# Whole weight rows with the step inside the staging tile, numerators beside keys, and weight passes tied behind chosen places of the first attention

## The chip, the cores and the metric

The kernel runs on one core of a Trainium2 chip. The metric is the device time of one execution in microseconds (us), median of several runs. The engines are called as the profile calls them: PE (TensorE matmul), PEld (its weight loads), DVE (VectorE), ACT (ScalarE), POOL (GpSimd) and SP (SyncE, which issues the loads here). The clock is PE's mean granted clock, 1.00 being full.

## The reference, cut to what matters

Four batches, four heads, 1088 positions, head size 32. An attention with squared sketch features gives `x` of 1088 x 128; a wave mixing multiplies its cosine and sine parts by two 1088 x 1088 weights.

```python
def phi(x):                                   # r = 8, so 64 features a head
    a = np.einsum('rd,bhsd->bhsr', S1, x)
    b = np.einsum('rd,bhsd->bhsr', S2, x)
    return np.einsum('bhsi,bhsj->bhsij', a, b).reshape(*x.shape[:-1], r * r)
num = phi(q) @ (phi(k)^T v)                   # shortened
den = phi(q) @ sum(phi(k)) + 1e-06
x = num / den
...
zr, zi = x * np.cos(x @ w_theta), x * np.sin(x @ w_theta)
y = np.einsum('ts,bsd->btd', w_tok_r, zr) + np.einsum('ts,bsd->btd', w_tok_i, zi)
u = x + y
return u + np.maximum(u @ w_ch, 0.0)
```

The weights arrive as float64 and are carried in as int64 bits. They must become f32 on the chip: 17 rows of 128 x 1088, each 8 bytes a value.

## The kernel before: the parts that matter

A weight piece is turned into f32 by three ACT passes and two DVE passes. ACT writes a scaled float of the high word, and beside it a 4-byte "step" made of an int16 (from the low word) and an f16 (from the high word); DVE shifts the float's bits by three and adds the step.

```python
def load_f32(dst, src):                       # PIECE = 544 columns
    st = stg.tile([P, PIECE], I64, tag="st", name="st")[:p, :n]
    nc.sync.dma_start(st, src)
    lo, hi = split(st)
    step = stg.tile([P, PIECE, 2], I16, tag="step", name="step", bufs=2)[:p, :n]
    x = dst.bitcast(I32)
    A.activation(dst, hi.bitcast(F32), AF.Copy, scale=2.0**-112)
    A.activation(step[:, :, 1].bitcast(F16), hi.bitcast(F32), AF.Copy, scale=2.0**-60)
    A.activation(step[:, :, 0], lo.bitcast(U32), AF.Copy, scale=2.0**-29)
    ts(x, x, 3, ALU.logical_shift_left)
    tt(V, x, x, step.rearrange("p n t -> p (n t)").bitcast(I32), ALU.add)
```

A scheduler puts the instructions of all stages in order on each engine by priority when the kernel is built.

```python
# ... end of the first attention, priority "first"
    query_slices(0); matrices(0); keys_values(0, spare); attention(0)
with level("attention"):
    keys(1); attention(1); keys(2)
mixing(0, True)
with level("attention"):
    attention(2); keys(3)
mixing(1, False)
# ... attention(3), mixing(2), mixing(3)
```

## Time and profile before

| | before |
|---|---|
| time, median (lowest to highest) | 358.53 us (357.6 to 360.12, 4 runs) |
| span, mean PE clock of the profiled run | 357.9 us, 0.877 |
| PE busy, DVE busy, ACT busy | 274.9, 250.4, 153.8 us |
| first mixing matmul | 115.87 us |
| last weight row ready | 117.4 us |
| second attention's denominators begin on DVE (fl) | 160.38 us |
| mixing of batch 1 begins | 189.55 us |

The last four rows of the table are milestones of the execution. One is fl, the first DVE instruction of the second attention that needs its features. This is it in the timeline of the kernel before (start, duration, engine, line, operation, tiles; in brackets the idle time before it and its releaser):

```profile
160.38 1.06 DVE L100 SCALAR_TENSOR_TENSOR fl<-lv 128x864 f32<-128x864 f32 x1 [2.07 <-ACT lv L449]
```

And this is the busy time on each side of it (PE, PEld, DVE, ACT, POOL, clock, DMA share, GB/s):

```profile
0.00:160.38 160.38, 90.69 (x447) 66.02 (x448) 124.57 (x405) 102.37 (x188) 0.70 (x6) 0.78 0.46 154
160.38:357.90 197.52, 184.19 (x910) 126.08 (x908) 125.88 (x309) 51.46 (x125) 0.00 (x0) 0.96 0.07 21
```

After fl, PE is busy for 184 of 197.5 us. Before it, no engine is: DVE for 125 and ACT for 102 of 160.

### The profile page before, as it was taken

The numbers are of one execution on the slowest core, as the hardware profiler recorded it, in microseconds if no ns is written. First come the engines' busy times: TensorE is split into PE (matmuls) and PEld (weight loads), VectorE is DVE, ScalarE is ACT, GpSimd is POOL, SyncE is SP. The second block draws the span as 40 slices with busy tenths as digits, with TensorE's granted clock in tenths as the row PEclk, the third lists the DMA queues.
The fourth block names the chain that finished last, engine by engine and source line by source line (L and its number), as shares of the span: only waits on it lengthen the run. The fifth ranks groups of instructions, "written<-read, shape, count | busy, mean of one in ns | idle before, by whom it ended". The sixth has DMA issues, their size and how long they took to land.

```text
span 357.9 us, 4021 instructions
## 1 busy us (share of the span) xinstructions
PE 274.9 (77%) x1355; PEld 192.1 (54%) x1355; DVE 250.4 (70%) x713; ACT 153.8 (43%) x313; POOL 0.7 (0%) x6
## 2 busy tenths in 40 slices
PE   0406680145327999999689999996999999999994
PEld 0304480023226676776357777674777766776562
DVE  4898886985996699559948794896589569542111
ACT  0799729997958442061134413312335131332000
POOL 0000000000000000000000000000000000000000
PEclk9999955556555899999969999997899999999998
DMA  7668447883720012020010122000000000000010
GB/s 289 214 229 269 153 145 243 293 304 108 238 59 4 2 65 69 0 67 3 22 40 2 65 66 70 21 22 20 0 0 3 0 9 15 22 20 0 0 44 18
DMA packets 11604, 28.78 MB, mean 80 GB/s; under 512 B 1216, under 2 KB 5568, under 8 KB 11584
## 3 DMA queue, kind: packets, MB, share of 16 engines
q1 hardware_dynamic: 11376, 28.51, 24.3%
q8 instruction: 10, 0.16, 0.2%
q14 instruction: 10, 0.08, 0.1%
q10 hardware_dynamic: 208, 0.02, 0.0%
HBM read 26.30 MB, written 2.23 MB: 80 GB/s over the span
## 4 chain that ended last, share of the span: by engine, by line
PE 69%; DVE 17%; ACT 8%; DMA 3%; issue 1%; ACTq 0%
PE y L566 36%; PE w L519 4%; PE acc L398 3%; ACT step L135 3%; PE w L539 2%; PE y L576 2%; PE y L398 2%; PE w L446 2%; ACT step L136 2%; DVE wT L93 2%; PE w L513 2%; PE w L388 2%; DMA s_t_st<-s_t 2%; PE acc L306 2%; PE w L447 2%; PE w L534 1%
## 5 line engine op out<-in xcount | busy, mean ns | idle before, releaser
L566 PE MATMUL y<-wT,zst 128*128 128x384 f32 (+1 forms) x384 | 134.8, 481 | 1.4 <-DVE zst L93 1.4
L566 PEld LDWEIGHTS y<-wT,zst 128*128 128x128 f32 x384 | 68.1, 193 | 30.6 <-DVE zst L93 2.3
L585 ACT COPY ot<-y 128x384 f32<-128x384 f32 (+2 forms) x16 | 6.0, 398 | 62.1 <-PE y L580 62.1
L135 ACT ACTIVATE step<-st 128x544 f16<-128x544 f32 (+1 forms) x35 | 27.8, 795 | 4.3 <-DVE wT L93 4.2
L93 DVE CUSTOM_DVE_ANT_0 wT<-wT,step 128x1088 uint16<-128x1088 uint16 x34 | 24.4, 718 | 5.8 <-ACT step L136 5.8
L519 PEld LDWEIGHTS w<-kvbd,qpT 128*128 128x128 f32 x144 | 21.6, 213 | 11.3 <-ACT qpT L517 10.4
L136 ACT ACTIVATE step<-st 128x544 int16<-128x544 uint32 (+1 forms) x35 | 27.4, 784 | 0.0
L519 PE MATMUL w<-kvbd,qpT 128*128 128x64 f32 x144 | 23.4, 297 | 3.2 <-ACT qpT L517 3.1
L134 ACT ACTIVATE wT<-st 128x544 f32<-128x544 f32 x34 | 22.9, 685 | 2.3 <-DMA st<-w_tok 2.2
L517 ACT COPY qpT<-w 128x256 f32<-128x256 f32 x36 | 12.9, 367 | 24.6 <-PE w L513 24.5
L513 PE MATMUL w<-ident,qp 128*128 128x128 f32 x72 | 14.6, 304 | 7.7 <-DVE qp L93 7.6
L93 DVE TENSOR_TENSOR uT<-xT,y 128x384 f32<-128x384 f32 (+1 forms) x12 | 6.3, 529 | 19.2 <-PE y L566 19.1
L97 DVE TENSOR_SCALAR tn<-w 128x384 f32<-128x384 f32 x12 | 6.7, 557 | 17.8 <-PE w L539 17.8
L536 ACT COPY xT<-w 128x384 f32<-128x384 f32 x12 | 5.7, 475 | 29.8 <-PE w L534 29.8
L449 ACT COPY lv<-w 128x384 f32<-128x384 f32 x36 | 14.9, 504 | 8.3 <-PE w L448 8.2
L513 PEld LDWEIGHTS w<-ident,qp 128*128 128x128 f32 x72 | 10.1, 170 | 9.8 <-ACT wT L134 8.1
L97 DVE TENSOR_SCALAR wT<-wT 128x544 int32<-128x544 int32 x34 | 14.6, 435 | 0.0
L446 PE MATMUL w<-mv,q 128*128 128x384 f16 x36 | 13.4, 372 | 0.8 <-DVE mv L93 0.8
L398 PEld LDWEIGHTS acc<-ld_v,kp 128*128 128x128 f32 x108 | 13.0, 192 | 1.5
L539 PEld LDWEIGHTS w<-w,xT 128*128 128x128 f32 x72 | 10.6, 215 | 5.2 <-ACT xT L536 4.5
L404 ACT COPY kvbd<-acc 64x64 f32<-64x64 f32 x6 | 1.2, 206 | 27.6 <-PE acc L398 27.6
L100 DVE SCALAR_TENSOR_TENSOR fl<-lv 128x864 f32<-128x864 f32 x4 | 4.2, 1054 | 12.3 <-ACT lv L449 12.3
(230 smaller groups left out, 523.5 us busy)
## 6 DMA issues: line engine op xcount, KB each, us to landing
st<-w_tok SPq DMA_DIRECT2D x34, 544.0 KB, 4.6
ld_k<-k_l SPq DMA_DIRECT2D x4, 576.0 KB, 4.0
ld_q<-q_l SPq DMA_DIRECT2D x4, 576.0 KB, 4.4
ld_v<-v_l SPq DMA_DIRECT2D x4, 576.0 KB, 3.8
out<-ot SPq DMA_DIRECT2D x8, 192.0 KB, 2.1
out<-ot SPq DMA_DIRECT2D x4, 128.0 KB, 1.8
st<-w_sq SPq DMA_DIRECT2D x1, 256.0 KB, 4.6
out<-ot SPq DMA_DIRECT2D x4, 32.0 KB, 1.8
```

The costliest lines, as they stand in the source:

```text
L93: eng.tensor_tensor(out=o, in0=a, in1=b, op=op)
L97: V.tensor_scalar(out=o, in0=a, scalar1=s1, scalar2=s2, op0=op0, **kw)
L134: A.activation(dst, hi.bitcast(F32), AF.Copy, scale=2.0**-112)
L135: A.activation(step[:, :, 1].bitcast(F16), hi.bitcast(F32), AF.Copy, scale=2.0**-60)
L136: A.activation(step[:, :, 0], lo.bitcast(U32), AF.Copy, scale=2.0**-29)
L398: nc.tensor.matmul(kv[:, n], kp[:, i * H + 2 * n:i * H + 2 * n + 2].rearrange("p h i j -> p (h i j)"), vn[:, c, 2 * n:2 * n + 2].rearrange ...
L446: nc.tensor.matmul(lp, q0, flat[:, 0:4 * W], start=True, stop=False, skip_group_check=True)
L449: A.copy(lv[:, :, :, c].rearrange("p l t n -> p (l t) n"), lp.rearrange("p (x n) -> p x n", n=HR))
L513: nc.tensor.transpose(tr[:, n * P:(n + 1) * P], qp[:, i * H + 2 * n:i * H + 2 * n + 2].rearrange("p h i j -> p (h i j)"), ident)
L519: nc.tensor.matmul(num[:, i * P + n * 2 * D:i * P + (n + 1) * 2 * D], qpT[:, n], kvbd[b][:, n], start=True, stop=True)
L539: nc.tensor.matmul(th[:, i * P:(i + 1) * P], xT[:, i * P:(i + 1) * P], w2[:, 0], start=True, stop=True)
L566: nc.tensor.matmul(yp[:, :t1 - t0], z, wT[:, i, t0:t1], start=(i == 0), stop=(i == NK - 1))
```

## The change

Its intent is to save instruction issues (whole rows in place of halves), to save memory (the step is written inside the staging tile), and to let PE begin the mixing earlier (half of the first batch's numerators runs beside its keys, and the weight passes on DVE are held behind places of the first attention). The core of the diff, cut:

```diff
-        st = stg.tile([P, PIECE], I64, tag="st", name="st")[:p, :n]
+        st = stg.tile([P, S], I64, tag="st", name="st")[:p, :n]
-        step = stg.tile([P, PIECE, 2], I16, tag="step", name="step", bufs=2)[:p, :n]
+        step = st.bitcast(I16).rearrange("p (n t) -> p n t", t=4)
         A.activation(dst, hi.bitcast(F32), AF.Copy, scale=2.0**-112)
+        A.activation(step[:, :, 0], lo.bitcast(U32), AF.Copy, scale=2.0**-29)
         A.activation(step[:, :, 1].bitcast(F16), hi.bitcast(F32), AF.Copy, scale=2.0**-60)
-        A.activation(step[:, :, 0], lo.bitcast(U32), AF.Copy, scale=2.0**-29)
         ts(x, x, 3, ALU.logical_shift_left)
-        tt(V, x, x, step.rearrange("p n t -> p (n t)").bitcast(I32), ALU.add)
+        rows.append(last_on_dve())
+        tt(V, x, x, lo, ALU.add)
+        rows.append(last_on_dve())
 ... # pool "stg": bufs 4 -> 3; key and query slices share one buffer; z of batch 0 has its own
-        query_slices(0)
-        matrices(0)
-        keys_values(0, spare)
-        attention(0)
+        matrices(0)
+        n_ready = tiles["ready", 0]
+        gates.extend([n_ready] * 2)
+        query_slices(0)
+        features_s(0)
+        denominator_slices(0, 1, 2)
+        keys_values(0, spare)
+        nums = [numerator(0, g, spare) for g in range(NG)]
+        features_n(0)
+        denominator_slices(0, 2, 3)
+        denominators(0)
+        gate(2)
+        d_ready = last_on_dve()
+        for g in range(NG):
+            mixed(0, g, nums[g])
+            gate(1 if g == 0 else NK)
+        for i, ins in enumerate(rows):
+            tc.add_manual_dep(ins, gates[i // 2].name, ...)
     with level("attention"):
-        keys(1)
+        with tc.issue_after(n_ready):
+            load(1, "kqv"); keys_powers(1); query_powers(1)
+        with tc.issue_after(d_ready):
+            keys(1)
```

Below, the *ties* are the `add_manual_dep` loop, and the *hold* is the pair of `issue_after` blocks.

## The prediction

> **What bounds the kernel now.** I read the page's busy table first, then its slices, then the start of the first mixing matmul in the timeline, then busy time by stretch, then the groups.
>
> The busy table and the slices (engine, then tenths of each 8.95 us):
>
> ```profile
> PE 274.9 (77%) x1355; PEld 192.1 (54%) x1355; DVE 250.4 (70%) x713; ACT 153.8 (43%) x313; POOL 0.7 (0%) x6
> ...
> PE   0406680145327999999689999996999999999994
> ...
> DVE  4898886985996699559948794896589569542111
> ACT  0799729997958442061134413312335131332000
> ```
>
> There are two stages. For about 13 slices (to 116 us) PE is idle more than half the time while DVE and ACT are loaded; after that PE is at 9 nearly everywhere. The border is the first matmul of the token mixing (line 566), in the timeline:
>
> ```profile
> 115.73 0.55 DVE L93 TENSOR_TENSOR zst<-x,tt 128x384 f32<-128x384 f32 x1
> 115.87 0.50 PEld L566 LDWEIGHTS y<-wT,zst 128*128 128x128 f32 x2 [1.42 <-DVE zst L93]
> 115.87 2.92 PE L566 MATMUL y<-wT,zst 128*128 128x384 f32 x4 [1.23 <-DVE zst L93]
> ```
>
> It waits for DVE (zst, end of the first attention's first group), not for a weight. The busy times by stretch (us, PE, PEld, DVE, ACT, POOL, PE clock, DMA share, GB/s) say what kept DVE:
>
> ```profile
> 60.00:70.00 10.00, 1.05 (x7) 0.69 (x6) 9.47 (x29) 9.93 (x17) 0.00 (x0) 0.50 0.87 309
> 70.00:80.00 10.00, 3.78 (x15) 2.11 (x16) 8.84 (x44) 9.98 (x17) 0.00 (x0) 0.50 0.85 298
> ...
> 90.00:100.00 10.00, 4.53 (x18) 3.63 (x18) 10.00 (x17) 8.71 (x17) 0.00 (x0) 0.50 0.61 198
> ...
> 120.00:130.00 10.00, 10.00 (x71) 7.76 (x71) 5.94 (x16) 4.19 (x9) 0.00 (x0) 1.00 0.00 0
> ```
>
> Before 116 us the conversion of the token weights (int64 bits to f32) shares DVE and ACT with the first attention. Its groups, 34 pieces of 544 columns for 17 weight rows:
>
> ```profile
> L135 ACT ACTIVATE step<-st 128x544 f16<-128x544 f32 (+1 forms) x35 | 27.8, 795 | 4.3 <-DVE wT L93 4.2
> L93 DVE CUSTOM_DVE_ANT_0 wT<-wT,step 128x1088 uint16<-128x1088 uint16 x34 | 24.4, 718 | 5.8 <-ACT step L136 5.8
> L136 ACT ACTIVATE step<-st 128x544 int16<-128x544 uint32 (+1 forms) x35 | 27.4, 784 | 0.0
> L134 ACT ACTIVATE wT<-st 128x544 f32<-128x544 f32 x34 | 22.9, 685 | 2.3 <-DMA st<-w_tok 2.2
> L97 DVE TENSOR_SCALAR wT<-wT 128x544 int32<-128x544 int32 x34 | 14.6, 435 | 0.0
> ```
>
> Later marks from the timeline: the last value that features(0) needs (mv) is ready at 77.6 us; mixing(0) ends on PE at 172.5; DVE starts the second attention's denominators (fl) at 160.4; mixing(1) starts at 189.55, and from there 168.3 us remain, nearly all PE.
>
> [...] four mixing matmuls take 2.92 us at 115.9, later ones 0.64 a pair, and the clock column reads 0.50 at 60 to 80.
>
> **The change, part by part.**
>
> 1. Whole rows. A row was six ACT instructions; in the timeline they start every 0.57, 0.67 and 0.65 us, so 2 x 1.89 = 3.8 us. Whole rows save three issues. [...] 3.6 us a row (estimate; [...] 4.1 if writing every 8 bytes is dearer). ACT total changes by 17 x 0.2 = 3 us only. DVE: 2 x (0.35 + 0.63) = 2.0 becomes 0.64 + 1.2 = 1.85 (estimate)[...].
>
> 2. Order. The instruction order of the changed kernel shows no weight pass on DVE until the first batch's numerator matrix is ready (call it N), then two rows, two around the end of the denominators, one after group 0 and twelve after that. Of the 33.5 us of weight passes (34 x 0.98, starts) some 21 sat before 77.6 us. Numerators beside keys put the half features, their slices and three qp products before N, and 36 numerator matmuls on PE. Walking the chain, with durations of the same operations in the timeline of before: s_t arrives 2 to 3 us earlier (it is issued ahead of q and v), so the scales are known near 14 us (14.7 now) and the key slices start at 15.6 (18.5 now) and take 5.3 (0.67 + 1.27 + 0.67 + 0.67 + 1.27, with small operations between): 20.9. The S matrices' cut (ten small, 1.8), their product and its scale (3.2) open PE's key sums at 26, which take 5.6 as now (31.3 to 37.3): 31.5. The query slices (4.7) and the cut of the key matrix (4) share DVE: 41. Half features on PE and ACT: 42. Then DVE has three kp (0.88 each), three qp (0.88), one batch column of slices (some 4) and the small operations of the matrix, paced by PE's transposes and products between them: 59. The last twenty dependent small operations cost 0.2 each: N = 63, if PE gets full clock after the half features. At half clock the 18 value and 36 numerator products (0.22 to 0.25 an instruction in place of 0.11 to 0.13) cost some 7 us more: N = 70.
>
> 3. From N: two rows (3.7), the rest of the denominators and two maxima of the next batch, 17 to 18 us of DVE: 81. Group 0 through x, theta, sine, zst: 10 us more. First mixing matmul near 91 to 92, 24 us earlier than now.
>
> 4. But the rows come later. With three staging buffers only rows 0 to 2 can pass ACT before N. Rows 3 and 4 follow at N + 8 to N + 15; row 5 stands behind the sine of group 0 on ACT (91), rows 6 and 7 behind the sines of groups 1 and 2. Row 7 ends near 105 and nine rows remain from 107. Each costs ACT 3.6 plus 0.5 of other work. The buffer loop is as long: add 1.3, DMA about 5.7 (4.6 for half the bytes; at 300 GB/s 0.56 MB more is 1.9), ACT 3.6, some DVE queueing, over three buffers 3.9. I take 4.2 a row: 9 x 4.2 = 38, so the last row is ready at E = 145.
>
> 5. After E. [...] the second attention's last matrix operations stand behind row 16's add: mixing(0)'s tail, one kp, the matrix, about 10.5 us; features on PE and ACT 5; then the denominators, 20 us of DVE as now (the key slices of batch 2 now stand inside them, because the shared slice buffer delays them), and 7 us of sine chain: mixing(1) at 145 + 42 = 187. Before: 189.55. The remainder is the same work in nearly the same order: 187 + 168 = 355 span, 1 us more by the clock.
>
> So of 24 us won at the start, 22 come back as a wait for weights and an exposed second attention. PE's idle time moves from before 116 us to 145 to 187.
>
> **The rivals.** (a) PE is the only bound from the first mixing matmul on: then the 24 us stay, 335. For it: PE at 9 after 116 us. Against: weights were finished by then; now they are not. [...] (b) [...] (c) PE stays cold through the numerators, N = 70: 362. For it: the 36 value matmuls at 46 to 54 us ran at half clock for 8 us without release; against: after the key sums (to 37 us) full clock held at half load until PE fell idle.
>
> **Range and chances.** The sum gives 355 to 356; a (partly) pulls down by 5 to 20, b and c push up by 6 to 8. I shade to 354, because every place of the ties looks chosen so that the model's mixing never starves, and I may have overdrawn the loop. Range 343 to 366. Faster than 351.7: 0.38; slower than 366: 0.12; between: 0.50.
>
> **What would show it.** First mixing matmul at 88 to 96 (part 3); whole-row ACT passes of 1.1 to 1.4 us and adds of 1.2 (part 1[...]); the last row's add at 140 to 150 and PE waiting for DVE's wT between 100 and 145 (part 4); PE mostly idle for 20 to 25 us before mixing(1), near 187 (part 5). The prediction is wrong if the rows end before 130 us, or if the second attention's features no longer wait for the last row.

The forecast's sum came to 355 to 356 us, shaded to 354. The slopes per column behind the 3.6 us a row put a 2-byte pass at 1.3 us, the branch of rival (a) ended at 350 us, and rival (b) made 364 us of dearer stores and a dearer add. The 4.1 us a row for dearer stores is a guess that names no source. The 3.6 can be followed from the kernel before: its ACT passes have a form of 256 columns beside that of 544, and the differences give 0.96 ns a column for f32 (409 and 685 ns) and 1.16 for the 2-byte outputs (460 and 793, 471 and 804). With 544 columns more, starts every 0.57, 0.67 and 0.65 us become 1.09, 1.30 and 1.28: 3.7 us a row (estimate).

## The result and the profile after

| | before | after |
|---|---|---|
| time, median (lowest to highest) | 358.53 us | 393.76 us (392.71 to 394.78, 4 runs) |
| span, mean PE clock | 357.9 us, 0.877 | 391.8 us, 0.843 |
| PE busy, DVE busy, ACT busy | 274.9, 250.4, 153.8 us | 293.7, 251.0, 191.3 us |
| first mixing matmul | 115.87 us | 95.65 us |
| last weight row ready | 117.4 us | 179.8 us |
| fl of the second attention | 160.38 us | 196.58 us |
| span after fl | 197.5 us | 195.2 us |

The changed kernel is 9.8% slower: ratio 1.0977, 95% interval 1.0927 to 1.1027. A ratio here is the mean time of one kernel's fast runs over that of the other's of the same rounds, so it is not quite the ratio of the medians.

First the page of the changed kernel: busy time, then tenths in 40 slices of 9.8 us, and PE's clock.

```profile
PE 293.7 (75%) x1382; PEld 203.2 (52%) x1382; DVE 251.0 (64%) x673; ACT 191.3 (49%) x263; POOL 0.7 (0%) x6
...
PE   2265889207967384467913999999799999999994
...
ACT  1997212596998999992611235051134341043000
...
PEclk9996655555898777858975799999999999999999
```

PE does start earlier, and then never gets going: its digits are ragged until about 215 us. In slices 10 to 17, counted from 0 (98 to 176 us), ACT stands at 9 nearly throughout. ACT's busy time grew by 37.5 us, though it has 50 instructions fewer. The groups name the growth (count, busy us, mean ns of one, idle us before them and releaser):

```profile
L145 ACT ACTIVATE st<-st 128x1088 int16<-128x1088 uint32 (+1 forms) x18 | 45.5, 2528 | 0.0
L146 ACT ACTIVATE st<-st 128x1088 f16<-128x1088 f32 (+1 forms) x18 | 45.4, 2520 | 0.3
L103 DVE CUSTOM_DVE_ANT_0 wT<-st,wT 128x2176 uint16<-128x2176 uint16 x17 | 21.9, 1289 | 21.7 <-ACT st L146 21.6
L144 ACT ACTIVATE wT<-st 128x1088 f32<-128x1088 f32 x17 | 20.6, 1209 | 4.4 <-DMA st<-w_tok 4.4
```

The f32 pass (L144) and the add (L103) cost about what was predicted (1.1 to 1.4 and 1.2), 1.2 and 1.3 us. The two 2-byte passes, L145 and L146, cost 2.5 us and not 1.1 to 1.4. The means mix in one short form of 256 columns; of the 17 full rows alone they are 2632 and 2624 ns. DVE waits 21.6 us for the second of them. The last row in the timeline shows the chain, and how an operation of the second attention (mxn) stands behind it:

```profile
95.65 1.65 PE L618 MATMUL y<-wT,zst 128*128 128x384 f32 x2 [1.59 <-DVE zst L103]
...
173.21 2.62 ACT L145 ACTIVATE st<-st 128x1088 int16<-128x1088 uint32 x1
...
175.86 2.62 ACT L146 ACTIVATE st<-st 128x1088 f16<-128x1088 f32 x1
...
177.23 0.27 PE L360 MATMUL acc<-ident,mn 128*1 128x128 f32 x1
178.51 1.29 DVE L103 CUSTOM_DVE_ANT_0 wT<-st,wT 128x2176 uint16<-128x2176 uint16 x1 [1.57 <-ACT st L146]
179.72 0.27 DVE L362 TENSOR_REDUCE mxn<-acc 1x4 f32<-1x128 f32 x1
...
196.58 1.06 DVE L110 SCALAR_TENSOR_TENSOR fl<-lv 128x864 f32<-128x864 f32 x1 [1.48 <-ACT lv L464]
...
223.56 0.91 PE L618 MATMUL y<-wT,zst 128*128 128x384 f32 x2
```

Row follows row every 6.1 to 6.2 us (the f32 pass of the last four starts at 153.59, 159.74, 165.95 and 172.09). The line at 223.56 is the first of batch 1's mixing. The span on each side of fl tells where the 33.9 us come from:

```profile
0.00:196.58 196.58, 121.58 (x520) 84.31 (x520) 126.27 (x369) 140.79 (x142) 0.70 (x6) 0.75 0.36 128
196.58:391.80 195.22, 172.12 (x862) 118.89 (x862) 124.73 (x305) 50.49 (x122) 0.00 (x0) 0.94 0.06 18
```

Before fl there are 36.2 us more (196.58 less 160.38), after it 2.3 fewer. DVE did the same work before fl (126 us against 125). ACT did 38 us more (141 against 102). So all of the loss lies before the second attention's denominators.

### The profile page after: what moved, and what is told of

Its sections match the earlier page's. It is cut to its first block, busy times and chain, and to the rows that moved or that the text cites. A ratio compares the mean times of both kernels' runs of the same rounds, so it can differ in the third digit from the quotient of the medians.

```text
span 391.8 us, 3966 instructions
## 1 busy us (share of the span) xinstructions
PE 293.7 (75%) x1382; PEld 203.2 (52%) x1382; DVE 251.0 (64%) x673; ACT 191.3 (49%) x263; POOL 0.7 (0%) x6
## 4 chain that ended last, share of the span: by engine, by line
PE 52%; ACT 26%; DVE 17%; issue 2%; DMA 2%; SPq 0%; ACTq 0%; DVEq 0%
PE y L618 24%; ACT st L145 9%; ACT st L146 9%; ACT wT L144 4%; PE acc L415 3%; PE w L566 2%; PE w L591 2%; PE w L560 2%; PE w L405 2%; PE y L415 2%; PE y L628 2%; DVE lv L103 2%; DVE wT L103 1%; DVE ksl L110 1%; DMA st<-w_tok 1%
## 5 line engine op out<-in xcount | busy, mean ns | idle before, releaser
L618 PE MATMUL y<-wT,zst 128*128 128x384 f32 (+1 forms) x408 | 154.2, 512 | 22.1 <-DVE wT L103 20.5
L146 ACT ACTIVATE st<-st 128x1088 f16<-128x1088 f32 (+1 forms) x18 | 45.4, 2520 | 0.3
L145 ACT ACTIVATE st<-st 128x1088 int16<-128x1088 uint32 (+1 forms) x18 | 45.5, 2528 | 0.0
L103 DVE CUSTOM_DVE_ANT_0 wT<-st,wT 128x2176 uint16<-128x2176 uint16 x17 | 21.9, 1289 | 21.7 <-ACT st L146 21.6
L144 ACT ACTIVATE wT<-st 128x1088 f32<-128x1088 f32 x17 | 20.6, 1209 | 4.4 <-DMA st<-w_tok 4.4
L103 DVE TENSOR_TENSOR uT<-xT,y 128x384 f32<-128x384 f32 (+1 forms) x12 | 6.4, 529 | 20.6 <-PE y L618 20.6
L405 PE MATMUL w<-s_bd,kT 128*128 128x64 f32 x72 | 11.6, 304 | 10.6 <-ACT kT L402 10.6
L405 PEld LDWEIGHTS w<-s_bd,kT 128*128 128x128 f32 x72 | 10.4, 214 | 15.8 <-ACT kT L402 15.3
L322 PE MATMUL acc<-ksl 128*128 128x384 f16 x27 | 10.9, 421 | 8.5 <-DVE ksl L110 8.5
L591 PE MATMUL w<-w,xT 128*128 128x128 f32 x72 | 12.9, 325 | 3.8 <-ACT xT L588 3.8
L103 DVE TENSOR_TENSOR zst<-x,tn 128x384 f32<-128x384 f32 (+2 forms) x16 | 7.0, 453 | 12.3 <-ACT tn L598 12.1
L472 PE MATMUL w<-mv,qsl 128*128 128x288 f16 (+2 forms) x45 | 12.7, 301 | 2.8 <-DVE qsl L107 2.8
```

The source lines that it names most:

```text
L103: eng.tensor_tensor(out=o, in0=a, in1=b, op=op)
L405: nc.tensor.matmul(kf[:, i * H * 2 * R:(i + 1) * H * 2 * R], kT[:, i], s_bd.rearrange("p h r -> p (h r)"), start=True, stop=True)
L472: nc.tensor.matmul(lp[:, 1:], q1, m[:, 0:3], start=False, stop=False, skip_group_check=True)
L591: nc.tensor.matmul(th[:, i * P:(i + 1) * P], xT[:, i * P:(i + 1) * P], w2[:, 0], start=True, stop=True)
L618: nc.tensor.matmul(yp[:, :t1 - t0], z, wT[:, i, t0:t1], start=(i == 0), stop=(i == NK - 1))
```

## The experiments

Eighteen kernels were run. Seventeen were timed in rounds together with the kernel before; b_stride was executed once. Theory 1 says that the way the step is stored costs the time; the rivals are the length of the rows, writing into the tile that is read, and the order with its ties.

### What makes the two passes slow

**b_inplace** is the kernel before with pieces of 544 and its own order; only the step goes inside the staging tile.

```diff
-        step = stg.tile([P, PIECE, 2], I16, tag="step", name="step", bufs=2)[:p, :n]
+        step = st.bitcast(I16).rearrange("p (n t) -> p n t", t=4)
 ... # low pass first, and the add takes lo, as in the change
```

> The kernel before, order and pieces of 544 unchanged, only the step stored inside the staging tile (one 2-byte value every 8 bytes, and the add reading it there). Theory 1: passes go from 0.79 to about 1.35 us (half of the 1088-column passes of the change), ScalarE gets 2 x 34 x 0.55 = 37 us more, about 20 of them before the first mixing matmul: 368 to 385 us. Theory 2 (length of rows): passes stay at 0.8 us, time within 1% of before.

Measured: 383.39 us (ratio 1.0678, 1.0633 to 1.0723). Its low-word pass, by form:

```profile
L135 ACT ACTIVATE st<-st 128x544 int16<-128x544 uint32 x34 | 48.5, 1427 | 0.0
```

1427 ns, where the same form took 793 in the kernel before. The length of the rows is out as the cause, and a small edit inside an otherwise unchanged kernel costs 25 us.

**b_stride** separates the two things that the edit does at once. The step has its own tile, so nothing is written where it is read, but the tile is spaced out to one 2-byte value every 8 bytes.

```diff
-        step = stg.tile([P, PIECE, 2], I16, tag="step", name="step", bufs=2)[:p, :n]
+        sd = stg.tile([P, PIECE, 2], I32, tag="sd", name="sd", bufs=2)[:p, :n]
+        step = sd.bitcast(I16)
```

> The kernel before with a step tile of its own, but written one 2-byte value every 8 bytes as in the change, not in place. If the 8-byte stride of the store is the cost: passes of 1.35 us at 544 columns. If writing into the tile that is read is the cost: 0.8 us.

Measured: 385.87 us in a single execution, so its state (fast or slow) is unknown. The pass is just as slow:

```profile
L136 ACT ACTIVATE sd<-st 128x544 int16<-128x544 uint32 x34 | 48.4, 1423 | 1.8 <-DVE wT L93 1.8
```

So it is the spacing of the stores: 1423 ns spaced in a tile of its own, 1427 spaced in place, 793 packed; a part of writing in place does not show. Between two forms of one kernel a column costs 1.16 ns with a 2-byte value every 4 bytes (460 ns at 256 columns, 793 at 544, in the kernel before) and 2.25 ns with one every 8 bytes (757 at 256, 2632 at 1088, in the changed kernel). Both edits also swap the two passes; e_sep and d_sep below keep the swap and pack the step, and there the passes take 1.4 us, so the swap is not the cause either.

### The change with a packed step, first attempt

**e_sep** keeps order, ties and whole rows and gives the step a tile of its own. The tile did not fit, so the key matrix's three tiles and one small one share the numerators' buffers.

```diff
-        step = st.bitcast(I16).rearrange("p (n t) -> p n t", t=4)
+        step = stg.tile([P, S, 2], I16, tag="step", name="step", bufs=2)[:p, :n]
-        tt(V, x, x, lo, ALU.add)
+        tt(V, x, x, step.rearrange("p n t -> p (n t)").bitcast(I32), ALU.add)
 ... # half, cm, cz and s2x: tag="feat", shared with the numerators' qp
```

> The changed kernel with its order, ties and whole rows, but the two 2-byte passes write a step tile of their own (pairs packed, one 2-byte value every 4 bytes) in place of the staging tile they read. Theory 1 (the way the step is stored costs the time): the two passes fall from 2.53 us to about 1.4 us [...], a row from 6.1 to about 4.0 us, some 13 rows times 2.1 gives 27 us back: 360 to 370 us, last row ready near 150 us. Theory 2 (length of the rows): the passes stay above 2.2 us and the time above 385 us. Theory 3 (order and ties are the loss, the passes beside it): passes fall to 1.4 us, time stays above 380 us.

The two forms of the kernel before (460 ns at 256 columns, 793 at 544) give 1.42 us at 1088.

Measured: 378.92 us (ratio 1.0521). The passes fell as expected:

```profile
L145 ACT ACTIVATE step<-st 128x1088 int16<-128x1088 uint32 x17 | 24.5, 1443 | 1.8 <-DVE wT L103 1.8
```

The time fell by 15 us and not by 27, so my own theory missed too.

**sep_noties** (the ties removed), **sep_old** (the first attention in the old order, no ties, no hold), **e_pieces** (544-column pieces in the changed order, ties kept) and **sep_early** (eight rows tied at the first place in place of two) all carry the same sharing of buffers.

```diff
-        for i, ins in enumerate(rows):                 # sep_noties: loop removed
-            tc.add_manual_dep(ins, gates[i // 2].name, ...)
-        gates.extend([n_ready] * 2)                    # sep_early
+        gates.extend([n_ready] * 8)
```

> The changed kernel with a step tile of its own (passes of 1.4 us, as the first of these runs showed) and without the ties. If what is left of the loss (379 against 358 us) comes from the ties, which put the rows between the links of the second batch's chain: the rows go early, the second batch's fl starts before 162 us and the time is 350 to 362 us. If it comes from the order (numerators beside keys, second batch's keys held until the denominators are done): 370 us or more, with the first mixing matmul later than 105 us.

> Whole rows and a step tile of its own, but the order of the kernel before for the first attention (numerators after keys, nothing held back, no ties). If whole rows as such do no harm: 352 to 362 us. If they are a part of the loss: above 366 us.

> The change with its order and ties, but the conversion of before: pieces of 544 columns, a step tile of its own. If whole rows save only three issues a row: within 2% of the run with whole rows and own step tile, 373 to 385 us. If whole rows are a loss through coarser hand-over to DVE and the loader: 360 to 370 us.

> The changed kernel with a step tile of its own and the first eight rows, not two, tied behind the numerator matrix alone; the others move up with them. If the rows' place is what delays the second attention: last row ready near 130 us in place of 141, fl of the second batch near 158, total 362 to 372 us. If the loader and ScalarE set the pace of the rows whatever the ties: within 1% of 379 us.

Measured: 376.55 us (1.0479), 378.14 us (one fast run at 371.82, three slow at 378 to 379), 400.54 us (1.1127) and 393.41 us (1.0951). e_pieces and sep_early met neither of their alternatives. sep_noties met the one that blames the order (370 us or more, first mixing matmul at 116.7 us) and sep_old the one that blames whole rows (above 366 us), but the clean versions below refute both readings (361.6 and 353.64 us). sep_old was the warning: it is close to the kernel before in everything but the rows, and its one fast run was 13 us slower. In all five kernels with shared buffers the span after fl is 209 to 215 us, against 195 to 199 in every kernel without them; of the 18 us between sep_old's fast run and d_old, 12 lie there. In sep_old and e_sep the half slices of batch 2 run 28 to 29 us after fl (189.89 against 160.97, and 196.09 against 168.21). In their clean versions they run 18 to 21 us after it (d_sep 187.30 against 169.59, d_old 175.32 against 154.58). The order in which the tiles take turns in the shared buffers puts the next half slices behind this attention's numerators; that this delay is the whole of the loss was not tested alone. These five runs show the cost of the passes and nothing safe about order. Whether pieces or whole rows are better in the changed order was not asked again.

### The same questions asked cleanly

**d_sep** writes the packed step of row i into row i+2 of the weights' own tile, which is not filled yet, with one spare row at the end. Only two small tiles of the first stage move, to buffers that are first used much later.

```diff
-    wT = const.tile([P, NK, S], F32, tag="wT", name="wT")
+    wT = const.tile([P, NK + 1, S], F32, tag="wT", name="wT")
-            load_f32(wT[:, i], w_tok[i])
+            load_f32(wT[:, i], w_tok[i], wT[:, min(i + 2, NK)])   # third: where the step goes
-        step = st.bitcast(I16).rearrange("p (n t) -> p n t", t=4)
+        step = step.bitcast(I16).rearrange("p (n t) -> p n t", t=2)
```

> The same question as the first run of this series, asked more cleanly: the memory for a step tile was found there by letting three tiles of the key matrix share the buffers of the numerators, which adds waits of its own. Here the step of row i is written, packed, into row i+2 of the weights' own tile, which is not yet filled, so no other tile changes its buffer. Changed order, ties, whole rows. If the 2-byte stores every 8 bytes are the whole error of the prediction: passes of 1.4 us, last row ready at 141 to 147 us, mixing of batch 1 at 184 to 190, total 352 to 360 us. If a second error sits after the last row: total 370 us or more, as in the first run.

Measured: one fast run at 360.0 us, three slow ones at 365.6 to 366.9 (median 365.68). The 2-byte passes, of the profiled run, which is a slow one:

```profile
L147 ACT ACTIVATE wT<-st 128x1088 f16<-128x1088 f32 x17 | 24.4, 1434 | 0.0
```

Set beside the change's 393.8, the packed step gives back 34 us by the one fast run. That is nearly all of the 35 us lost against the kernel before. With fast runs on both sides, the pair a_free and d_free below gives 31 us.

**d_noties** takes the ties away, **d_free** the ties and the hold, **d_old** also restores the old order of the first attention (whole rows and the earlier loads of the sketch matrices S1 and S2 stay).

```diff
-        with tc.issue_after(d_ready):                  # d_free, d_old
-            keys(1)
+        keys(1)
```

> The same with the ties taken away. If the ties pay for themselves once the step is packed: slower than the run with ties, 362 us or more. If they cost: 345 to 355 us.

> The same with neither the ties nor the hold on the second batch's loads, scales and keys; only the order numerators beside keys is left, with whole rows. If that order is worth the 20 us that the first mixing matmul gained: 340 to 352 us. If the rows in front of the first attention take it back: 355 to 365 us.

> Whole rows with packed step, first attention in the order of the kernel before, no ties, no hold. Against the run of the same order with the shared buffers (378 us): if those buffers were the loss, 352 to 362 us; if whole rows or the changed S loads are, 370 us or more.

Measured: d_noties 361.6 us (ratio 1.009, 1.006 to 1.012), d_free 353.87 us (0.9878, 0.9848 to 0.9909), d_old 353.64 us (0.9872, 0.9833 to 0.9911). The last two are correct and beat both kernels, by 1.2 to 1.3% against before: less than the 2% that counts as a difference here, but their intervals lie below 1. The order "numerators beside keys" adds nothing to d_old, which does not have it. d_old met its first alternative; d_noties and d_free fell between theirs.

### The second error, and what sets the time

**d_keys** is d_sep without the hold. **a_free** has the change's spaced-out step, but neither ties nor hold. **a_noties** lacks the ties alone. **d_late** and **d_late2** leave the first ten or six rows free and tie the rest, without the hold.

```diff
-        for i, ins in enumerate(rows):
+        for i, ins in list(enumerate(rows))[2 * 10:]:   # d_late; 2 * 6 in d_late2
```

> The changed kernel without the ties of the rows to places of the first attention; in-place step as in the change. Theory 1 (cost of a row on ScalarE): ScalarE has the same 17 rows of 6.1 us, which now start earlier, so the second attention is less exposed, but the first attention is held up: first mixing matmul after 105 us, total 375 to 392 us. Theory 3 (ties are the loss): under 362 us.

> Packed step, order and ties of the change, but the second batch's loads, scales and keys are not held back. If the hold is the second error: last row at 140 to 145 us as before, fl of batch 1 by 160 us, 350 to 357 us. If the ties are: within 1% of the fast run with both (360 us) or above.

> In-place step as in the change, whole rows, numerators beside keys, but neither ties nor hold. If the two errors add up: 354 (the same with packed step) plus 28, less what ScalarE has free early: 375 to 385 us. If ties and hold only hurt because the rows are slow: under 365 us.

> Packed step, no hold, rows 0 to 9 free and rows 10 to 16 tied behind the first attention's second group. If DVE's share of the rows before the first mixing matmul is what that matmul pays for: first mixing matmul near 107 us (120 without ties, 94 with all), no row missed by PE, 345 to 351 us. If the time is set by DVE's sum of work up to the second attention wherever the rows stand: 353 to 357 us.

> The same with only rows 0 to 5 free and 6 to 16 tied. First theory: first mixing matmul near 101 us, some waits of PE for rows, 347 to 354 us. Second theory: 353 to 360 us.

Measured: a_noties 390.19 us (1.0867), d_keys 359.37 us (355.7 to 360.3, ratio 1.0029), a_free 384.99 us (1.0725), d_late 359.12 us (1.0008), d_late2 368.57 us (1.0271). a_noties and a_free met the expectations that rest on the cost of the passes. d_keys fell short of what the hold was to give: its median is within 1% of d_sep's one fast run (360.0), and only its fastest run, the profiled one, lies in the range given to the hold. Taking away ties or hold alone (361.6, 359.37) gains nothing that these runs show; without both it is 353.87. Both late versions missed: tying the last rows costs 5 and 15 us against d_free and gains nothing. Without ties and hold the spaced-out step costs 31 us (384.99 less 353.87), so the errors do about add up.

The table puts the profiled runs side by side by the start of their first mixing matmul. Times are in us; the last column is the span less fl.

| run | step | first mixing matmul | last row ready | fl | span | after fl |
|---|---|---|---|---|---|---|
| d_sep (slow) | packed | 93.6 | 143.3 | 169.6 | 365.2 | 195.6 |
| d_keys | packed | 95.4 | 140.8 | 157.3 | 353.6 | 196.3 |
| after | spaced | 95.7 | 179.8 | 196.6 | 391.8 | 195.2 |
| d_late2 | packed | 106.4 | 145.2 | 171.3 | 366.5 | 195.2 |
| d_late | packed | 111.2 | 135.1 | 162.1 | 357.2 | 195.1 |
| before | packed | 115.9 | 117.4 | 160.4 | 357.9 | 197.5 |
| d_noties | packed | 116.4 | 106.2 | 161.4 | 359.7 | 198.3 |
| d_old | packed | 118.9 | 97.7 | 154.6 | 352.0 | 197.4 |
| d_free | packed | 120.1 | 106.9 | 155.3 | 351.8 | 196.5 |
| a_noties | spaced | 140.2 | 143.8 | 189.2 | 388.6 | 199.4 |
| a_free | spaced | 145.0 | 141.4 | 186.3 | 383.2 | 196.9 |

The first mixing matmul ranges over 51 us and the span does not follow it: d_keys begins 25 us before d_free and ends 2 us after it in its fastest run, 5.5 us by the medians. The span is fl plus 195 to 199 us in all eleven (the five kernels with shared buffers are left out). So the question becomes what sets fl. Two probes on d_old, wrong in their result, take work from one engine alone: **d_noshift** drops the 17 shifts on DVE, **d_noact** drops both 2-byte passes of each row on ACT (the add becomes a subtraction of the row from itself, still 1285 ns).

```diff
-        ts(x, x, 3, ALU.logical_shift_left)             # d_noshift
-        A.activation(step[:, :, 0], lo.bitcast(U32), AF.Copy, scale=2.0**-29)               # d_noact
-        A.activation(step[:, :, 1].bitcast(F16), hi.bitcast(F32), AF.Copy, scale=2.0**-60)
```

> Wrong result on purpose: the packed-step kernel with the first attention in the old order (353.6 us), without the left shift of each row: 17 x 0.72 = 12 us of DVE less, nothing else. If DVE's work sets the second attention's start: fl moves from 154.6 to 143 to 148 us and the total to 342 to 347 us. If ScalarE or the dependent chain does: 351 to 355 us.

> Wrong result on purpose: the same kernel (shift kept) without the two 2-byte passes of each row, the add taking the row itself: 17 x 2.85 = 48 us of ScalarE less, DVE about as before. If ScalarE sets the second attention's start: fl moves by tens of us, total 315 to 340 us. If DVE does: 349 to 355 us.

Measured: d_noshift 346.3 us, d_noact 350.0 us (d_old: 353.64); both are what the texts give for DVE. The busy times up to fl, first of d_old, then of d_noshift, then of d_noact, in the columns used above:

```profile
0.00:154.58 154.58, 80.92 (x428) 59.27 (x429) 118.84 (x344) 96.99 (x131) 0.70 (x6) 0.78 0.44 159
```

```profile
0.00:144.76 144.76, 79.41 (x428) 58.62 (x429) 109.19 (x327) 97.29 (x131) 0.70 (x6) 0.79 0.48 170
```

```profile
0.00:149.71 149.71, 85.61 (x438) 63.03 (x439) 119.47 (x350) 55.78 (x101) 0.70 (x6) 0.79 0.43 164
```

With 9.7 us less on DVE (118.84 to 109.19) fl comes 9.8 us earlier: one for one. With 41.2 us less on ACT (96.99 to 55.78) it comes 4.9 us earlier: one for eight. In d_old fl is therefore set in the main by DVE's work. That this holds whatever the order is not shown: the eight kernels of the table with a packed step have 119 to 126 us of DVE up to fl, but fl ranges from 154.6 to 171.3, so how long DVE waits counts too (32.6 us in d_keys, 47.4 in d_late2). With the spaced-out step ACT has 139 to 141 us up to fl, against 97 to 102. a_free and d_free differ by that step and the places of two small tiles, and fl moves by 31 us.

## Why the prediction was wrong, point by point

Predicted were 354 us, range 343 to 366, with a chance of 0.12 for more than 366; 393.8 came.

**What bounds the kernel now: right in its parts, wrong in its emphasis.** The wait at 115.87 us is real, but it is not the one that sets the end. d_keys removes 20 us of it and ends as the kernel before does (359.37 us).

**Part 1, whole rows: this step failed.** The f32 pass (1.2 us) and the add (1.29 against 1.2) were right. Each 2-byte pass was put at 1.3 us. Stores packed at 4 bytes come near that (1.41 to 1.45 us at 1088 columns in d_old and d_sep), but the figure was used for stores spaced at 8. The line said in the same breath that these might be dearer, and allowed 4.1 us a row in place of 3.6. They measured 2.63 us each, and a row 6.1. A hint stood in the prediction's own profile: the 2-byte passes, which store every 4 bytes, took 795 and 784 ns where the f32 pass took 685. Of rival (b), the DVE half did not appear (the add took 1289 ns reading a 4-byte word every 8 bytes, 1286 with the packed step of d_sep), and the ACT half was right in kind and five times too small (0.5 us a row allowed, 2.5 came).

**Part 2, order: near.** The numerator matrix was ready at 66.7 us (63 predicted, 70 with PE at half clock). PE's clock stood at 0.50 between 50 and 100 us, so rival (c) was partly true.

**Part 3: near.** The first mixing matmul came at 95.65, with 91 to 92 predicted.

**Part 4, the rows come later: the mechanism was right, its size carries the failure on.** E was to be 145; the last row was ready at 179.8, 35 us later. d_sep, with packed stores and the same ties, had it at 143.3 (slow profile; 140.8 in d_keys, fast, without the hold): with passes of 1.43 to 1.45 us, close to the 1.3 assumed, its E is right. One term of the buffer loop is added up wrongly: 4.6 and 1.9 us of DMA are 6.5 and not 5.7 (5.0 was measured), without harm to the 4.2.

**Part 5: right for the changed kernel.** From E to the mixing of batch 1 took 43.8 us (42 predicted; it starts at 223.56), and 168.2 remained (168 predicted). The predicted 355 plus 34.8 for E plus 1.8 here gives 391.6, and the span is 391.8. The 42 us do not hold everywhere: with E near 145, as predicted, they are 44 in d_keys but 53 in d_sep and d_late2 (see the second error).

**A second, smaller error** was hidden by the first. In d_sep fl came 26 us after the last row, with some 15.5 predicted (10.5 for the tail and the matrix, 5 for the features). The key-value products there are slow. First two groups of them from the changed kernel (granted clock 1.00, 0.12 us a product), then one from d_sep (0.22 us a product, as in the kernel before from 46 to 54 us at a clock of 0.50: 26 in 5.79 us):

```profile
184.54 1.67 PE L415 MATMUL acc<-ld_v,kp 128*128 128x64 f32 x14
186.38 1.23 PE L415 MATMUL acc<-ld_v,kp 128*128 128x64 f32 x10
```

```profile
153.67 5.22 PE L416 MATMUL acc<-ld_v,kp 128*128 128x64 f32 x24
```

With the groups after these, 36 products take 7.9 us in d_sep and 4.5 in the changed kernel: this is some 3 of the 11 us, and where the rest goes was not followed. d_late2, a fast one, shows the same: fl 26 us after the last row, and the same 24 products in 5.22 us. What this error costs the change is not settled: the span was to be 355 us, and d_sep's was 358.3 in its one fast run and 363.9 to 365.2 in the slow ones. Whether the hold has a part in it is not shown either: d_late2 has no hold, and d_keys, without it, has fl at 157.3 but in the fastest of its five runs.

Rival (a), 335 us, is refuted. In eleven kernels the start of the first mixing matmul moved over 51 us, and the span did not follow it.

## What to carry to other kernels

When an edit changes where a pass writes, price the store by its spacing: find an instruction of the same spacing in a trace, or time one, before the old slope is used. Look for the milestone after which the span is constant in several versions of the kernel (here fl), and spend effort only on the engine whose work moves it; here an early start of the busiest engine was worth nothing when that milestone stayed (d_keys against d_free: first mixing matmul 25 us earlier, fl 2 us later). A probe on one order says nothing sure about another. When memory for an experiment is found by sharing buffers, the sharing is a second change: check it with a run that should be neutral.
